# Attention and experts in one Trainium2 kernel: a quarter of the turned blocks copied on GpSimd, the first pair unturned, and a new order of the attention's instructions

## The chip, the core and the metric

The kernel runs on one core of a Trainium2 chip. The metric is the device time of one execution in microseconds, lower is better. The core's engines work through instruction streams of their own, each in order: PE (TensorE, matmuls), DVE (VectorE), ACT (ScalarE), POOL (GpSimd) and SP (SyncE), which here issues the DMA transfers. They wait for each other by semaphores.

## The reference

Attention with pooled queries (4 batches, 8 heads, 1152 keys, 576 queries after pooling pairs, head size 64), whose output is the input of a mixture of 8 experts with weights from a Sinkhorn iteration.

```python
q_pool = q.reshape(B, H, S // 2, 2, D).mean(axis=3)
scores = (1.0 / np.sqrt(D)) * np.matmul(q_pool, k.transpose(0, 1, 3, 2))
attn = np.exp(scores - np.max(scores, axis=-1, keepdims=True))
attn = attn / (np.sum(attn, axis=-1, keepdims=True) + 1e-09)
x = np.matmul(attn, v)                       # then (B * S/2, H * D) = (2304, 512)
...
P = np.exp(logits - logits.max())            # logits = x @ w_gate
for _ in range(8):                           # rows, then columns, normalized
    P /= P.sum(1, keepdims=True) + 1e-09
    P /= P.sum(0, keepdims=True) + 1e-09
    P *= N / E
for e in range(E):
    out += P[:, e:e + 1] * (np.maximum(x @ w1[e], 0.0) @ w2[e])
```

## The kernel before

The attention comes first, then the experts (`moe`, which the change leaves alone).

The attention takes two heads of a batch together, a pair; there are 16 pairs, p = 0 to 15. The 576 queries of a pair are five units: t = 0 to 3 of 128 queries for each of the two heads, and one mixed unit (t = 4) that holds the last 64 queries of both. A unit m = 5p + t goes through these steps, each a function under `unit_ops`:

- `qk` (PE, L462): scores into the PSUM tile `S`, in three parts of 384 keys; an unmixed part is six matmuls (three products of split operands, two heads). `S` has two buffers.
- `out_max` (DVE, L470): each part scaled, copied into the SBUF tile `E` and its row maximum taken; this frees `S`. `neg` (L476) takes the maximum of the three.
- `expo` (ACT, L486): the exponential in place, with row sums into `rs`.
- From here E has to be laid with keys on partitions. For most units `tr` (PE, L513, into the PSUM tile `tr`, three buffers) transposes 128x128 blocks, and `tr_out` copies them to `ET` on ACT (L523) or DVE (L525); then `av` (PE, L542) multiplies with v into the PSUM tile `av` (one buffer). The units t = 0 and 1 of the pairs 0 to 14 go another way, the turned way: `turn` (DVE, L496) transposes 32x32 blocks within each group of 32 partitions into the tile `turned`; 16 transfers `front` (SP, L554) move each of the 4x4 block quarters of 32 partitions to its place in `fronted`, four of them from a group of partitions to the same group; and `av_turned` (PE, L563) multiplies `fronted` with v, for both units in one matmul of 256 columns. Its columns are left in another order (a, t, j) in PSUM; `x_out` (ACT, L579) reads them out in the order (t, a, j), and the other two units' with a second instruction (L581). `turned` and `fronted` exist once each, so the turns of pair p + 1 need the transfers of pair p to have read, and these need `av_turned` of the pair before to be done.

Once a pair, `rec` (DVE, L588 to L591) adds 1e-9 to the nine row sums, inverts them and turns them; `spread_out` and `spread_in` carry them through DRAM to all partitions, and `x_scale` (POOL) multiplies the result. `pair_ops` loads q, k, v and splits q and k into two parts for the products (POOL additions, ACT copies).

None of this is issued in the order of the code. Each step is put into `Plan` with an engine, a cost in ns, a priority (a place in time, in units of `UNIT`), what it reads and writes, and the buffers it takes. `Plan.order` runs a list schedule over these numbers: whenever an engine is free it takes the step with the least priority value of those that are ready by its reckoning, and the engines' streams come out in that order. `STICK` favours PE steps of the same kind (`mode`) as the one before; `WAIT` is how long an engine may be held for a better step. So numbers in the table decide the streams, and on the chip each engine then follows its stream strictly.

Of the kernel before, what the change touches and what calls it, by code (L numbers as in the profile page):

```python
# [11 lines left out]
P = 128  # L12
# [151 lines left out]
class Plan:  # L164
# [9 lines left out]
    WAIT = 150  # L174
# [32 lines left out]
    def order(self):  # L207
# [31 lines left out]
        while len(out) < n:  # L239
            moved = False  # L240
            for e in engines:
# [30 lines left out]
                if e == "PE":  # L272
                    if mode and mode != o["mode"]:
                        gap = GAP_R if o["mode"] == "R" else GAP
                    mode = o["mode"]
# [35 lines left out]
TR0 = 10.0  # L311
TD = 30.0
STICK = 4.0
GAP = 145
GAP_R = 195
# [3 lines left out]
TURNED = 2  # L319

# [9 lines left out]
def attention(tc, q, k, v, w_gate, xx, ident, wg, PR, blocks, wt, dry=False, NP=NPAIRS):  # L330
# [11 lines left out]
    if not dry:  # L342
# [17 lines left out]

    def sbt(shape, dt, tag):
        return sb.tile(shape, dt, name=tag, tag=tag, bufs=caps[tag])
# [4 lines left out]
    def op(eng, cost, prio, r=(), w=(), new=(), use=(), lat=0, mode="", after=0):  # L367
        def put(fn):
            plan.op(eng, cost, prio, fn, r, w, new, use, lat, mode, after)
        return put  # L370

    def pair_ops(p):
# [6 lines left out]
        for j, (lo, hi) in enumerate(qparts):  # L379
            @op("SP", 600, T - 16 + 0.15 * j, w=[("q", p, j)], new=[] if j else [(("qr", p), "qr")], use=[("qr", p)] if j else [],  # L380
                lat=2000 + 500 * j)
# [5 lines left out]
        for j, (lo, hi) in enumerate(kparts):  # L387
            @op("SP", 600, T - 15.9 + 0.1 * j, w=[("k", p, j)], new=[] if j else [(("kr", p), "kr")],
                use=[("kr", p)] if j else [], lat=2000 + 500 * j)
# [5 lines left out]
        @op("SP", 600, T - 6, w=[("v", p)], new=[(("v", p), "vt")], lat=4000)  # L395
# [39 lines left out]
    def unit_ops(m):  # L435
# [10 lines left out]
        turns = t < TURNED and p < NP - 1  # L446
# [42 lines left out]
        if turns:  # L489
            for h in heads:  # L490
# [4 lines left out]
                def turn(h=h):  # L495
                    nc.vector.transpose(turned[:, :, :, h, t].rearrange("p b c j -> p c b j"), D["E", m][:, h].rearrange("p (c b j) -> p c b j", b=4, j=BK))  # L496
# [30 lines left out]
        new_av = t in (TURNED if p < NP - 1 else 0, QT)  # L527
        w = 64 if mixed else P
        of = t * P if not mixed else 0

        for j in range(3):
            @op("PE", 12 * (29.5 if mixed else 54.5), T + TR0 + 2.6 + 0.7 * j, mode="C",
                r=[("v", p)] + [("ET", m, g) for g in range(-(-nb // 4))],
                w=[("av", p, mixed)], new=[(("av", p, mixed), "av")] if new_av and j == 0 else [],
                use=[("v", p), ("ET", m)] + ([] if new_av and j == 0 else [("av", p, mixed)]))
            def av(j=j):
                if new_av and j == 0:
                    D["av", p, mixed] = pst([P, 512], "av")
                for c in range(3 * j, 3 * j + 3):
                    for h in range(2):  # L540
                        x = D["ET", m][:, c, 64 * h:64 * h + 64] if mixed else D["ET", m][:, h * NC + c]
                        nc.tensor.matmul(D["av", p, mixed][64 * h:64 * h + 64, of:of + w], D["v", p][:, h, c, :], x,  # L542
                                         start=(c == 0), stop=(c == NC - 1))

        if t == QT - 1 and p < NP - 1:
            @op("SP", 1, T - UNIT * (QT - 1) + 14, r=[("Y", p, i, h) for i in range(TURNED) for h in range(2)], w=[("F", p)], new=[(("F", p), "F")], use=[("T", p)])
            def room():
                pass

            for a in range(4):  # L550
                for z in range(4):
# [343 lines left out]
```

## Time and profile before

| | us |
|---|---|
| median of three runs (lowest, highest) | 1946.83 (1944.96, 1949.51) |
| the profiled execution's time | 1945.41 |
| its span, first to last instruction | 1943.5 |
| PE busy | 1910.2 (98%) |
| DVE busy | 1482.4 (76%) |
| ACT busy | 832.1 (43%) |
| POOL busy | 432.3 (22%) |

The span is what the profile's rows divide up; the time also holds what lies around it. A busy time is the union of an engine's instructions. PE's instructions overlap and their ends are modelled, so 98% says that PE nearly always had something in flight, not that it ran at its peak. The chain that ended last follows the work back from the end, at each step to what released it.

### The profile page before, as it was taken

How to read it: one execution, taken by the hardware profiler on the slowest of the kernel's cores; microseconds unless marked ns; L12 is line 12 of the kernel's file. 1: busy time of each engine (PE TensorE's matmuls, PEld its weight loads, DVE VectorE, ACT ScalarE, POOL GpSimd, SP SyncE). 2: the span in 40 equal slices, each digit the busy share in tenths (PEclk: the TensorE clock that was granted, in tenths of full speed). 3: DMA queues.
4: the chain of work that ended last, by engine and by line, in shares of the span. 5: the costliest groups of instructions: out<-in, count | busy, mean ns of one | idle time of the engine just before them, and what ended most of it. 6: DMA issues, size and time to landing. Idle time of an engine off the chain costs nothing.

```text
span 1943.5 us, 30922 instructions
## 1 busy us (share of the span) xinstructions
PE 1910.2 (98%) x11957; PEld 1681.8 (87%) x11957; DVE 1482.4 (76%) x2976; ACT 832.1 (43%) x1423; POOL 432.3 (22%) x442
## 2 busy tenths in 40 slices
PE   7999999999999999999999999999999999999999
PEld 5777777788999999999899999999989999999997
DVE  8888889878987777777867777777786777776764
ACT  5666776675433333333333333333344333333331
POOL 3222232211022212121322212121232212122210
PEclk7999999999999999999999999999999999999999
DMA  7666666522222121121312121222222121221211
GB/s 231 184 161 168 184 173 169 124 70 83 86 76 76 55 76 65 66 68 63 109 66 77 55 76 65 66 74 68 77 87 77 65 66 65 66 81 61 77 50 39
DMA packets 63221, 177.02 MB, mean 91 GB/s; under 512 B 12768, under 2 KB 22624, under 8 KB 63072
## 3 DMA queue, kind: packets, MB, share of 16 engines
q1 hardware_dynamic: 62784, 174.63, 30.3%
q8 instruction: 94, 1.54, 0.3%
q14 instruction: 55, 0.45, 0.1%
q10 hardware_dynamic: 288, 0.39, 0.1%
HBM read 134.81 MB, written 4.79 MB: 72 GB/s over the span
## 4 chain that ended last, share of the span: by engine, by line
PE 84%; DVE 8%; DMA 4%; SPq 2%; ACT 1%; issue 1%; POOL 0%; DVEq 0%; ACTq 0%
PE pso L792 39%; PE psh L754 12%; PE psh L752 12%; PE psh L753 12%; PE S L462 4%; PE av L563 3%; DVE E L470 2%; SPq L554 2%; DVE turned L496 2%; PE tr L513 2%; PE av L542 2%; DMA fronted<-turned 1%; DMA vt<-in_v_dram 1%; DVE rs L588 1%; DVE w1l L149 0%
## 5 line engine op out<-in xcount | busy, mean ns | idle before, releaser
L752 PE MATMUL psh<-xch,w1h 128*128 128x384 f32 x1344 | 451.1, 336 | 2.9 <-ACT p L767 1.5
L754 PE MATMUL psh<-xch,w1l 128*128 128x384 f32 x1344 | 449.6, 336 | 0.6 <-DVE w1l L149 0.6
L792 PE MATMUL pso<-w2h,hl 128*128 128x512 f32 x1152 | 450.1, 391 | 0.0
L792 PE MATMUL pso<-w2l,hh 128*128 128x512 f32 x1152 | 450.1, 391 | 0.0
L753 PE MATMUL psh<-xcl,w1h 128*128 128x384 f32 x1344 | 450.1, 335 | 0.0
L792 PE MATMUL pso<-w2h,hh 128*128 128x512 f32 x1152 | 448.6, 389 | 0.0
L761 ACT ACTIVATE hh<-c 128x384 fp32r<-128x384 f32 x384 | 199.8, 521 | 278.6 <-DVE c L772 277.4
L802 DVE SCALAR_TENSOR_TENSOR x<-pso,PR,x 128x512 f32<-128x512 f32 x264 | 196.9, 746 | 151.1 <-PE pso L792 150.6
L130 POOL TENSOR_TENSOR w1t<-w1s 128x256 f32<-128x256 f32 x88 | 67.0, 761 | 1031.2 <-DMA w1s<-in_moe_w_dram 836.6
L752 PEld LDWEIGHTS psh<-xch,w1h 128*128 128x128 f32 x1344 | 252.4, 188 | 9.1 <-ACT p L767 2.2
L753 PEld LDWEIGHTS psh<-xcl,w1h 128*128 128x128 f32 x1344 | 252.4, 188 | 3.5
L792 PEld LDWEIGHTS pso<-w2h,hl 128*128 128x128 f32 x1152 | 216.2, 188 | 45.1
L792 PEld LDWEIGHTS pso<-w2h,hh 128*128 128x128 f32 x1152 | 216.5, 188 | 43.1 <-ACT hh L761 0.5
L754 PEld LDWEIGHTS psh<-xch,w1l 128*128 128x128 f32 x1344 | 252.2, 188 | 1.7 <-DVE w1l L149 1.4
L792 PEld LDWEIGHTS pso<-w2l,hh 128*128 128x128 f32 x1152 | 216.3, 188 | 43.0
L470 DVE TENSOR_SCALAR_CACHE_REDUCE E<-S 128x384 f32<-128x384 f32 x432 | 219.6, 549 | 34.6 <-PE S L462 33.8
L159 ACT ACTIVATE w2h<-w2s 128x1024 fp32r<-128x1024 f32 x96 | 101.9, 1062 | 279.2 <-PE pso L792 181.3
L762 DVE SCALAR_TENSOR_TENSOR hl<-c,hh 128x384 fp32r<-128x384 f32 x384 | 211.4, 551 | 3.9 <-ACT hh L761 2.9
L486 ACT ACTIVATE E<-E,st 128x1152 f32<-128x1152 f32 x144 | 180.0, 1253 | 74.6 <-DVE st L476 70.8
L462 PE MATMUL S<-kT,qT 64*128 64x384 f32 (+1 forms) x1296 | 179.6, 372 | 22.4 <-DVE E L470 19.1
L160 DVE TENSOR_TENSOR w2l<-w2s,w2h 128x1024 fp32r<-128x1024 f32 x96 | 136.8, 1425 | 84.4 <-ACT w2h L159 84.4
L767 ACT ACTIVATE p<-psh 128x384 f32<-128x384 f32 x96 | 47.2, 491 | 331.5 <-PE psh L754 331.1
(89 smaller groups left out, 2194.6 us busy)
## 6 DMA issues: line engine op xcount, KB each, us to landing
w1s<-in_moe_w_dram SPq DMA_DIRECT2D x96, 512.0 KB
w2s<-in_moe_w_dram SPq DMA_DIRECT2D x96, 512.0 KB
fronted<-turned SPq DMA_DIRECT2D x240, 144.0 KB
qr<-in_q_dram SPq DMA_DIRECT2D x15, 640.0 KB
vt<-in_v_dram SPq DMA_DIRECT2D x16, 576.0 KB
kr<-in_k_dram SPq DMA_DIRECT2D x15, 576.0 KB
out_dram<-x SPq DMA_DIRECT2D x18, 256.0 KB
RB<-rd SPq DMA_DIRECT2D x32, 128.0 KB
```

Of the source, the lines that this page charges most:

```text
L159: self.nc.scalar.activation(out=hi, in_=self.raw2[k], func=ACTF.Copy)
L160: self.nc.vector.tensor_tensor(out=lo, in0=self.raw2[k], in1=hi.bitcast(F32), op=ALU.subtract)
L462: nc.tensor.matmul(ps[:, h, :PK], D["qT", p][rows, x, t * P:(t + 1) * P], D["kT", p][rows, y, j * PK:(j + 1) * PK], start=(i == 0), stop=( ...
L470: nc.vector.tensor_scalar(out=D["E", m][:, h, j * PK:(j + 1) * PK], in0=D["sc", m, j][:, h, :PK], scalar1=0.0625, scalar2=None, op0=ALU.mu ...
L486: nc.scalar.activation(out=x, in_=x, func=ACTF.Exp, bias=D["st", m][:, h, 3:4], accum_out=D["rs", p][:, col + h * QT:col + h * QT + 1])
L752: nc.tensor.matmul(ps, hi[:, a, c, :], blocks.xch[:, b, c, :], start=(c == 0), stop=False)
L753: nc.tensor.matmul(ps, hi[:, a, c, :], blocks.xcl[:, b, c, :], start=False, stop=False)
L754: nc.tensor.matmul(ps, lo[:, a, c, :], blocks.xch[:, b, c, :], start=False, stop=(c == 1))
L761: nc.scalar.activation(out=hh[:, fh, ts], in_=src, func=ACTF.Relu)
L762: nc.vector.scalar_tensor_tensor(out=hl[:, fh, ts], in0=src, scalar=0.0, in1=hh[:, fh, ts].bitcast(F32), op0=ALU.max, op1=ALU.subtract)
L792: nc.tensor.matmul(ps, u[:, fh, ms], w[:, fh, :], start=(n == 0), stop=(n == 11))
L802: nc.vector.scalar_tensor_tensor(out=a, in0=ps, scalar=PR[:, m, e:e + 1], in1=a, op0=ALU.mult, op1=ALU.add)
```

## The change

What it does, part by part:

- Pairs 0 and 15 go the ordinary way; only the pairs 1 to 14 have their units t = 0 and 1 turned (`spins`).
- Of the 16 quarters the four that stay on their partitions (`stay`, z = a) are copied by GpSimd; twelve transfers remain (`front`). The tiles are now `T` and `F`, taken anew for each pair from a pool with one buffer each.
- `av_turned` writes PSUM in the order (t, a, j): 256 columns in eight runs of 32. `x_out` is then one plain copy.
- 1e-9 is added by ACT (`eps`); `rec` on DVE starts with the reciprocal.
- `av` and `av_turned` are one step each for the list (three before), so nothing is put between their parts.
- The list's numbers: the loads' and transfers' costs, that a buffer read by a transfer is free only when the transfer has landed, `WAIT`, the gaps, `UNIT`, and a table `OFF` of shifts to the priorities by the step's name.

```diff
-    WAIT = 150
+    WAIT = 0
...
-                    last_use[name] = max(last_use.get(name, 0.0), end + self.FREE)
+                    last_use[name] = max(last_use.get(name, 0.0), end + self.FREE + o["lat"] * (o["eng"] == "SP"))
...
-UNIT, MIXED = 4.0, 1.8
+UNIT, MIXED = 7.6, 6.0
...
+OFF = dict(rec=20.5, q_add=-8.0, room=-38.0, qk=-2.0, stay=60.0, eps=-3.5, av_turned=43.0, expo=-12.0, spread_out=-12.0,
...
-        turned = low.tile([P, 4, NC, 2, TURNED, BK], F32, name="turned")
-        fronted = low.tile([P, 4, NC, 2, TURNED, BK], F32, name="fronted")
...
+    def done(p):
+        return [(("av", p, False), t) for t in ((0, *range(TURNED, QT)) if 0 < p < NP - 1 else range(QT))]
+
+    def lowt(tag):
+        return low.tile([P, 4, NC, 2, TURNED, BK], F32, name=tag, tag=tag, bufs=caps[tag])
...
-            plan.op(eng, cost, prio, fn, r, w, new, use, lat, mode, after)
+            plan.op(eng, cost, prio + OFF.get(fn.__name__, 0), fn, r, w, new, use, lat, mode, after)
...
-        turns = t < TURNED and p < NP - 1
+        spins = 0 < p < NP - 1
+        turns = t < TURNED and spins
...
+            if t == TURNED - 1:
+                @op("Pool", 1, T + 8, r=[("Y", p, i, h) for i in range(TURNED) for h in range(2)], w=[("G", p)], new=[(("F", p), "F")], use=[("T", p)])
+                def room():
+                    D["F", p] = lowt("F")
+
+                def runs(y, a, z):
+                    return y[BK * a:BK * a + BK, z].rearrange("p c h t j -> p (c h t j)")
+
+                for a in range(4):
+                    @op("Pool", 1300, T + 8 + a, r=[("G", p)], w=[("Z", p, a, a)], use=[("T", p), ("F", p)])
+                    def stay(a=a):
+                        nc.gpsimd.tensor_copy(runs(D["F", p], a, a), runs(D["T", p], a, a))
+
+                    for z in range(4):
+                        if z != a:
+                            @op("SP", 700, T + 8 + 0.1 * (4 * a + z), r=[("G", p)], w=[("Z", p, a, z)], use=[("T", p), ("F", p)], lat=2500)
+                            def front(a=a, z=z):
+                                nc.sync.dma_start(out=runs(D["F", p], z, a), in_=runs(D["T", p], a, z))
...
-                            nc.tensor.matmul(D["av", p, False][64 * h:64 * h + 64, :TURNED * P], D["v", p][:, h, c, :],
-                                             fronted[:, :, c, h].rearrange("p a t j -> p a (t j)"), start=(c == 0), stop=(c == NC - 1))
...
+                        nc.tensor.matmul(D["av", p, False][64 * h:64 * h + 64, :TURNED * P].rearrange("p (t a j) -> p a t j", a=4, j=BK), D["v", p][:, h, c, :],
+                                         D["F", p][:, :, c, h], start=(c == 0), stop=(c == NC - 1))
...
-                nc.scalar.activation(out=y[:, i:], in_=A[:, i:n], func=ACTF.Copy)
+                nc.scalar.activation(out=xx[:, hp, o:o + n], in_=D["av", p, mixed][:, :n], func=ACTF.Copy)
...
+            def eps():
+                y = D["rs", p][:, :2 * QT + 1]
+                nc.scalar.activation(out=y, in_=y, func=ACTF.Copy, bias=1e-9)
...
-                nc.vector.scalar_tensor_tensor(out=y, in0=y, scalar=1e-9, in1=y, op0=ALU.add, op1=ALU.max)
```

What the new numbers do to the streams shows at three places. The first is PE between two pairs, in the middle of the attention: the last unit's transposes (`tr<-ident,E`), the scores (`S<-kT,qT`), the products (`av<-ET,vt`) and the turned product (`av<-fronted` before, `av<-F` now). Before, then now:

```order
L513 MATMUL tr<-ident,E 128x128 x12
L462 MATMUL S<-kT,qT 128x384 x12
L542 MATMUL av<-ET,vt 64x128 x18
L462 MATMUL S<-kT,qT 128x384 x12
L513 MATMUL tr<-ident,E 128x128 x10
L462 MATMUL S<-kT,qT 128x384 x6
L513 MATMUL tr<-ident,E 128x128 x5
L542 MATMUL av<-ET,vt 64x128 x18
L462 MATMUL S<-kT,qT 128x384 x12
L563 MATMUL av<-fronted,vt 64x256 x18
L462 MATMUL S<-kT,qT 128x384 x12
L542 MATMUL av<-ET,vt 64x64 x18
```

```order
L542 MATMUL tr<-ident,E 128x128 x12
L470 MATMUL S<-kT,qT 128x384 x12
L542 MATMUL tr<-ident,E 128x128 x6
L571 MATMUL av<-ET,vt 64x128 x18
L581 MATMUL av<-F,vt 64x4x2x32 x18
L470 MATMUL S<-kT,qT 128x384 x12
L542 MATMUL tr<-ident,E 128x128 x9
L470 MATMUL S<-kT,qT 128x384 x12
L571 MATMUL av<-ET,vt 64x128 x18
L470 MATMUL S<-kT,qT 128x384 x12
```

The turned product now follows a product directly, the run of six scores is gone, and the fourth unit's product comes after the turned one. (A matmul of this list is one or two in the trace.)

The second place is SP in one pair of the middle: the transfers of the turned blocks, the loads of v, q and k, and the row sums' way through DRAM (`rd`, `RB`). Before, then now:

```order
L554 DMA fronted<-turned 32x1152 x3
L398 DMA vt<-in_v_dram 128x1152
L554 DMA fronted<-turned 32x1152 x13
L385 DMA qr<-in_q_dram 128x1280
L597 DMA rd<-rt 9x32 x4
L393 DMA kr<-in_k_dram 128x1152
```

```order
L525 DMA F<-T 32x1152 x12
L405 DMA vt<-in_v_dram 128x1152
L615 DMA rd<-rt 9x32 x4
L400 DMA kr<-in_k_dram 128x1152
L392 DMA qr<-in_q_dram 128x1280
```

The twelve transfers go out together and the load of v comes behind them.

The third is DVE in one pair of the middle, from the row sums to the turns (`T<-E` is the turn now). Before, then now:

```order
L588 SCALAR_TENSOR_TENSOR rs_80<-rs_80 128x9
L589 RECIPROCAL rs_80<-rs_80 128x9
L591 STREAM_TRANSPOSE rt<-rs_80 128x32
L470 TENSOR_SCALAR E,st<-S 128x384 x2
L496 STREAM_TRANSPOSE turned<-E 128x9x4x32
L470 TENSOR_SCALAR E,st<-S 128x384 x3
L496 STREAM_TRANSPOSE turned<-E 128x9x4x32
```

```order
L607 RECIPROCAL rs_81<-rs_81 128x9
L609 STREAM_TRANSPOSE rt<-rs_81 128x32
L478 TENSOR_SCALAR E,st<-S 128x384 x3
L484 TENSOR_REDUCE st<-st 128x2
L478 TENSOR_SCALAR E,st<-S 128x384
L554 COPY ET<-tr 128x512
L478 TENSOR_SCALAR E,st<-S 128x384 x4
L506 STREAM_TRANSPOSE T<-E 128x9x4x32
L484 TENSOR_REDUCE st<-st 128x2
L506 STREAM_TRANSPOSE T<-E 128x9x4x32 x3
```

Before, each turn has maxima around it; now three of the four stand in a row.

## Rows read from the trace of the kernel before

**Rows 1.** Windows by stage: busy us (instructions) of each engine, clock, DMA share, GB/s.
```profile
46.76:72.78 26.02, 24.76 (x272) 19.74 (x274) 24.37 (x71) 17.96 (x33) 7.20 (x4) 1.00 0.66 172
...
229.04:253.50 24.46, 24.46 (x272) 19.74 (x274) 21.94 (x71) 17.97 (x33) 10.21 (x6) 1.00 0.70 184
...
443.74:1943.50 1499.76, 1492.10 (x7497) 1349.69 (x7497) 1102.73 (x1836) 532.20 (x895) 307.65 (x363) 1.00 0.22 70
```

**Rows 2.** Chain that ended last, 0 to 450: start us, us, what.
```profile
63.40 2.67 DVE rs L588
...
72.78 4.04 PE av L563 x36
...
229.04 4.04 PE av L563 x36
...
253.50 4.04 PE av L563 x36
...
363.41 2.72 PE tr L63 x32
...
414.59 4.06 PE av L563 x36
```

**Rows 3.** The same chain, between the turned products of two pairs.
```profile
125.21 5.72 PE av L563 x36
...
141.87 5.26 DMA fronted<-turned
147.79 1.38 DVE turned L496
...
153.18 4.04 PE av L563 x36
```

**Rows 4.** Timeline of SP's DMA queue in that stretch.
```profile
130.98 1.80 SPq L554 DMA_DIRECT2D fronted<-turned  x3
...
133.83 8.81 SPq L554 DMA_DIRECT2D fronted<-turned  x13
```

**Rows 5.** Groups by line and form, 46.76 to 414.59: busy us, mean ns; idle before.
```profile
L433 POOL TENSOR_TENSOR kT<-kr,kT 128x1152 fp32r<-128x1152 f32 x13 | 34.9, 2688 | 20.3 <-ACT kT L428 20.3
...
L525 DVE COPY ET<-tr 128x512 f32<-128x512 f32 x44 | 30.2, 687 | 2.6 <-PE tr L513 2.5
...
L588 DVE SCALAR_TENSOR_TENSOR rs<-rs 128x9 f32<-128x9 f32 x14 | 14.7, 1053 | 0.0
...
L579 ACT ACTIVATE x<-av 128x256 f32<-128x256 f32 x14 | 5.4, 384 | 31.2 <-PE av L563 31.2
L581 ACT ACTIVATE x<-av 128x256 f32<-128x256 f32 x14 | 5.3, 379 | 0.0
```

**Rows 6.** Chain in the shortest period, 229.04 to 253.50.
```profile
233.08 1.27 PE S L462 x12
234.34 1.20 PE av L542 x36
...
238.86 0.52 PE S L462 x3
...
240.04 1.45 PE S L462 x8
241.49 1.31 PE tr L513 x12
...
244.06 2.12 PE av L542 x36
...
248.68 0.72 PE S L462 x6
```

**Rows 7.** Groups by line, 0 to 400: GpSimd's fills.
```profile
masks.py:197 POOL MEMSET ident<- 128x128 f32 x1 | 0.2, 204 | 0.3 <-POOLq L880 0.3
L356 POOL MEMSET rs<- 128x32 f32 x2 | 0.2, 124 | 0.0
```

**Rows 8.** Windows in the start, columns as in rows 1.
```profile
20.00:25.00 5.00, 3.43 (x18) 2.09 (x16) 4.72 (x12) 2.40 (x4) 3.11 (x4) 0.50 1.01 410
```

More of the change, by code (lines that the diff above doesn't have):

```diff
@@ L379, in pair_ops @@
         for j, (lo, hi) in enumerate(qparts):
[L380 to L381 removed]
+            @op("SP", 600 if first else 2600, T - 16 + 0.15 * j, w=[("q", p, j)], new=[] if j else [(("qr", p), "qr")], use=[("qr", p)] if j else [],
+                lat=2000)
             def load_q(j=j, cs=slice(lo, hi)):
@@ L525, in tr_out @@
                     nc.vector.tensor_copy(o, i)
-        new_av = t in (TURNED if p < NP - 1 else 0, QT)
+        t0 = QT if mixed else TURNED if spins else 0
+        new_av = t == t0
         w = 64 if mixed else P
         of = t * P if not mixed else 0
[L531 to L539, printed above, removed]
-                    for h in range(2):
-                        x = D["ET", m][:, c, 64 * h:64 * h + 64] if mixed else D["ET", m][:, h * NC + c]
-                        nc.tensor.matmul(D["av", p, mixed][64 * h:64 * h + 64, of:of + w], D["v", p][:, h, c, :], x,
-                                         start=(c == 0), stop=(c == NC - 1))
@@ new lines, in unit_ops, with av @@
+        A0 = ("av", p, mixed)
+        @op("PE", 36 * (29.5 if mixed else 54.5), T + TR0 + 2.6, mode="C",
+            r=[("v", p)] + [("ET", m, g) for g in range(-(-nb // 4))] + ([] if new_av else [(A0, t0)]), w=[(A0, t)],
+            new=[(A0, "av")] if new_av else [], use=[("v", p), ("ET", m)] + ([] if new_av else [A0]))
+        def av():
+            if new_av:
+                D["av", p, mixed] = pst([P, 512], "av")
+            for c in range(NC):
+                for h in range(2):
+                    x = D["ET", m][:, c, 64 * h:64 * h + 64] if mixed else D["ET", m][:, h * NC + c]
+                    nc.tensor.matmul(D["av", p, mixed][64 * h:64 * h + 64, of:of + w], D["v", p][:, h, c, :], x,
+                                     start=(c == 0), stop=(c == NC - 1))
@@ new lines, in unit_ops, with av_turned @@
+        if t == QT - 1 and spins:
+            @op("PE", 36 * 53.5 * TURNED, T - UNIT * (QT - TURNED) + TF, mode="C",
+                r=[("v", p), (A0, TURNED)] + [("Z", p, a, z) for a in range(4) for z in range(4)],
+                w=[(A0, 0)], use=[("v", p), ("F", p), A0])
+            def av_turned():
+                for c in range(NC):
+                    for h in range(2):
+                        nc.tensor.matmul(D["av", p, False][64 * h:64 * h + 64, :TURNED * P].rearrange("p (t a j) -> p a t j", a=4, j=BK), D["v", p][:, h, c, :],
+                                         D["F", p][:, :, c, h], start=(c == 0), stop=(c == NC - 1))
+                if p == NP - 2:
+                    low.release()
+                    blocks.place(tc)
@@ L649, in attention @@
         T = PAIR * NP
-        src = [("x", p) for p in range(2 * NPAIR)] + [("av", NP - 2, False)]
+        src = [("x", p) for p in range(2 * NPAIR)] + done(NP - 2)
         for n, i in enumerate((0, 1, 2, 3, 4, 6, 5)):
```

60 lines of the change are left out of this document (21 added, 39 removed).

## The prediction

> **What bounds the kernel now.** I read three views: the windows by stage, the chain that ended last, and the groups by line. The windows show that the expert stage, 443.74 to 1943.50, is PE's alone: 1492.10 of 1499.76 us busy [rows 1]. The change doesn't touch it, so all that can move lies in the 443.74 us ahead of it, the attention.
>
> There the chain shows where each turned product (`av<-fronted`) begins; there are 15, one for each of the pairs 0 to 14, and the distance from one to the next is the period of a pair: (414.59 - 72.78) / 13 = 26.29 us on the mean, and 253.50 - 229.04 = 24.46 us in the shortest [rows 2]. In that shortest one PE is busy for all of its 24.46 us, VectorE for 21.94, ScalarE for 17.97 [rows 1]. So a pair's own work on PE is 24.46 us and the other 1.8 us are waits. Two kinds stand in the chain.
>
> The first is a loop through the two buffers of the turned blocks. A turned product ends at 125.21 + 5.72 = 130.93 [rows 3]. Only then is the destination free: SP issues three transfers at 130.98, then a load of v, then thirteen from 133.83 to 142.64 [rows 4]. What waits last for them ends at 141.87 + 5.26 = 147.13; only then may VectorE overwrite the source: the next turn begins at 147.79, and the next turned product at 153.18 [rows 3]. From end to begin that is 22.25 us; with the 4.04 us of a product at full clock the loop gives 26.3 us, the mean period.
>
> The second is SCALAR_TENSOR_TENSOR on the row sums: 2.67 us on the chain at 63.40 [rows 2], 1053 ns on the mean of 14 and 14.7 us in all [rows 5], for nine columns. It sits on VectorE until ScalarE's last sum is there, with the maxima for PE's next scores queued behind it.
>
> **The sum.** It is made against the profiled execution: 1943.50 us of span, 1945.41 us of time; the median of the three runs is 1.42 us above that.
>
> *PE's own work in a pair.* The order shows the 72 paired score matmuls in six runs of 12 instead of seven runs (12, 12, 6, 12, 12, 6, 12; the run of 9 in the trace is three single-headed and six paired). Twelve take 1.27 us, six take 0.72 alone, nine take 1.45 of which three are 0.52 [rows 6]; seven runs are 5 x 1.27 + 0.72 + 0.93 = 8.0, six are 7.6. The 45 transposes and three ordinary products stay, and the turned product now follows another product. So 24.46 - 0.4 = 24.0 us.
>
> *VectorE in a pair.* It loses the SCALAR_TENSOR_TENSOR. The rest stays, so some 21.6 of 24.0 us: still less than PE. The order puts the turns together, the last three in a row: 4 x 1.38 = 5.5 us [rows 3] in which no maximum is made. Meanwhile PE has six transposes (half of twelve), a product and the turned product, 0.7 + 2.12 + 4.04 = 6.9 us [rows 2, 6], none of which needs VectorE. Margin 1.4 us. If that cover is gone, each us by which the turns are late is one of PE's.
>
> *The loop.* Twelve transfers in place of 16, with no load between them: 16 took 142.64 - 130.98 = 11.7 us, so 0.7 us each, and twelve 7.6 to 8. The loop shrinks by some 3.7 us to 18.5 + 4.04 = 22.6 us, under PE's 24.0: it no longer decides.
>
> *GpSimd's four copies.* No row shows a copy of 32 partitions on GpSimd. Below: filling 128 and 32 columns takes 204 and 124 ns [rows 7], 0.83 ns a column, so 1152 columns 1.1 us. Above: a two-input operation over 1152 columns takes 2688 ns [rows 5]. I take 1.6, nearer the fill, since one input is read and not two. GpSimd's 7.20 us in a pair [rows 1] become 11.6 to 18; either end is under 24. The copies lie beside the twelve transfers, of which the last lands about 12.5 us after the issue begins (8 and the 147.13 - 142.64 = 4.5 of the last one now); at 2.7 us each, with one addition over 640 columns that the order puts among them (1.5 at the same rate), they end at 12.3. So they cost nothing unless one takes over (24.0 - 7.2) / 4 = 4.2 us.
>
> *The ScalarE edits.* Adding 1e-9 there costs some 0.2 us, and two copies of the result (384 and 379 ns [rows 5]) become one; ScalarE has 6 us of idle in a pair. Nothing.
>
> *Waits that stay.* The new list still ties three in-order engines together. I take 0.4 us a pair (0 at best, as in the shortest pair now; 1.2 at worst, two thirds of today's 1.8). So a period of 24.4.
>
> *The start.* Up to the turned product of pair 1, at 72.78 now. VectorE is busy for nearly all of it; it loses four turns (5.5), the wait in the SCALAR_TENSOR_TENSOR (2.5), and gains copies out of PSUM: by the order six of 512 and three of 256 columns in place of five of 512, 687 ns for one of 512 [rows 5] and about 0.4 for one of 256: +1.8. Net -6.2. PE gains 36 transposes (3 x 1.31) and two products (2 x 2.12), loses a turned product (4.04), and leaves one product and six score matmuls for later: +1.4. [...] With transposes to do while VectorE works, PE stands idle less; I can't tell when the clock will rise. Bounds: 0 (it stays low as long as now, and the added work runs at half speed) to -9. I take -5.5: 67.3.
>
> *The end.* The last period now already holds work of pair 15; the new list has it behind the turned product of pair 14. By the order, 30 score matmuls (3.2), 27 transposes (2.9) and one product (2.12) move there: 8.2. Now it is 443.74 - 414.59 = 29.15 us; less some 0.5 of waits that I let go: 36.8. In turn the 13 periods lose nine transposes (1.0) and six score matmuls (0.6), and hold the gate's products, 2.72 [rows 2] and 0.3 for their transposes, once: 13 x 24.4 + 3.0 - 1.6 = 318.6.
>
> Together 67.3 + 318.6 + 36.8 = 422.7, in place of 443.74: 21.0 us less. 1945.4 - 21.0 = 1924.4, and against the median 1.4 more: **1926**, 1.1% faster.
>
> [...] The permutation that ScalarE did on its way out of PSUM is now PE's: 256 columns are accumulated in eight runs of 32 in place of one run. ScalarE's read in this pattern costs 384 ns against 379 without [rows 5], 1%; no row shows PE writing so. [...]
>
> **The rivals.**
> 1. *Slower: the scattered accumulation costs.* Turned products are 14 of 14 on PE's path, with nothing beside them. The upper price from rows: were each run of 32 charged like the smallest product here (36 of 64 columns in 1.20 us [rows 6], 33 ns), a matmul of eight runs would take 267 ns in place of 112 and the product 9.6 us: 14 x 5.6 = 78, 2004 us. It decides from 21.0 / 14 = 1.5 us more for a product of 4.04. [...] 6%.
> 2. *New waits for the old.* The margins are thin (1.4 us at the turns; scores have two buffers), and VectorE is at 90%. Then a period near 25.4 in place of 24.4: 1939. For it: only one of 13 periods is free of waits today. Against it: that one had VectorE at 21.94 of 24.46, which is as full. 15%.
> 3. *The loop is not cut:* transfers land as late as now because loads take their place on the same queues, or something else holds the buffers. Then 26.0 again: 67.3 + 13 x 26.0 + 1.1 + 36.8 = 443.2, which is today's 443.74 and the time 1946. Against it: a quarter of the bytes is gone. 4%.
> 4. *GpSimd becomes the bound,* at over 4.2 us for a copy. At 5, 27.2 us a pair: 1926 + 13 x 2.8 = 1962. The row of 2688 ns is against it. 3%.
>
> **Chances and range.** The forecast has 72%; its own range is 1918 (no waits, start at -9) to 1934 (0.8 us of waits a pair, start at -2). A measurement here tells 0.2%, 3.9 us, from no change. Faster by more: 72 + 14 from rival 2 = 86%. Within: 5% (rival 3 and the tail of 2). Slower: 9% (1 and 4). The range 1918 to 1941 leaves out rivals 1, 3 and 4, and what is faster still.
>
> **What would show it.** Right: `av<-F` begin 24.2 to 24.8 us apart and take 4.04 each; the first expert product at 420 to 426; turns that never wait for a transfer; RECIPROCAL that starts with no wait. [...]

## The result and the profile after

The changed kernel takes 1915.23 us (median of five runs, 1914.44 to 1916.61); the kernel before, beside it, 1949.51 (1944.96 to 1954.04). The ratio is 0.9827, 95% interval [0.9808, 0.9846]: 1.7% faster. The forecast was 1926 with a range of 1918 to 1941: the sign was right, and the time lies below the range; the span fell by 30.1 us (1943.5 to 1913.4) where I had worked out 21.0.

The profiled execution took 1915.23 us with a span of 1913.4 us. First the windows by stage of the kernel after (columns as in rows 1): the stretch of the thirteen periods, one period, the experts.

```profile
64.33:377.58 313.25, 313.25 (x3531) 257.88 (x3532) 278.01 (x899) 232.76 (x415) 147.88 (x102) 1.00 0.60 154
182.88:206.81 23.93, 23.93 (x274) 19.84 (x272) 21.38 (x71) 18.07 (x32) 11.62 (x8) 1.00 0.63 163
413.92:1913.40 1499.48, 1491.82 (x7497) 1349.34 (x7497) 1100.00 (x1836) 533.32 (x895) 308.19 (x363) 1.00 0.22 70
```

The experts take 1499.48 us, 0.28 less than in [rows 1]; all the rest of the difference lies ahead of them. PE is busy for all of the 313.25 us between the first and the last turned product. The timeline of the kernel after, with rows of PE, then one pair on DVE, SP and POOL:

```profile
11.48 2.29 PE L470 MATMUL S<-kT,qT 64*128 64x384 f32 x12 [0.51 <-DVE E L478]
...
17.60 0.66 PE L542 MATMUL tr<-ident,E 128*128 128x128 f32 x4
18.19 0.80 PE L470 MATMUL S<-kT,qT 64*128 64x384 f32 x6
...
21.24 1.31 PE L470 MATMUL S<-kT,qT 64*128 64x384 f32 x12
...
64.33 4.11 PE L581 MATMUL av<-F,vt 128*64 128x256 f32 x36
...
158.95 4.05 PE L581 MATMUL av<-F,vt 128*64 128x256 f32 x36
182.88 4.05 PE L581 MATMUL av<-F,vt 128*64 128x256 f32 x36
...
377.58 4.05 PE L581 MATMUL av<-F,vt 128*64 128x256 f32 x36
...
413.92 0.45 PE L772 MATMUL psh<-xch,w1l 128*128 128x384 f32 x1 [0.23 <-DVE w1l L149]
...
157.64 1.37 DVE L506 STREAM_TRANSPOSE T<-E 128x1152 f32<-128x1152 f32 x1
...
158.97 4.14 DVE L506 STREAM_TRANSPOSE T<-E 128x1152 f32<-128x1152 f32 x3
...
163.18 8.74 SPq L525 DMA_DIRECT2D F<-T  x12
...
163.23 1.14 POOL L519 COPY F<-T 32x1152 f32<-32x1152 f32 x1 [4.33 <-PE av L581]
...
165.95 3.52 POOL L519 COPY F<-T 32x1152 f32<-32x1152 f32 x3
```

Turned products stand 182.88 - 158.95 = 23.93 us apart (26.29 before on the mean, [rows 2]) and take 4.05; ten of the thirteen periods are 23.93 to 23.96, the first two 25.08 and 21.63, the one with the gate's products 27.10. The last three turns (158.97 to 163.11) run beside the product (158.95 to 163.00); twelve transfers and four copies begin as both end, and the next product comes 19.9 us later. Before, two of the four turns stood between the landing of the transfers and the product, at 147.79 [rows 3] and 150.02. Twelve scores take 2.29 us at 11.48 and 1.31 at 21.24, and six take 0.80 at 18.19: PE comes to full speed at about 17.6 us, where it was granted half from 20 to 25 us [rows 8].

Groups by form in the kernel after, 46.76 to 377.58 (columns as in rows 5); the POOL row holds all the copies:

```profile
L506 DVE STREAM_TRANSPOSE T<-E 128x1152 f32<-128x1152 f32 x53 | 70.9, 1364 | 2.0 <-ACT E L494 0.5
...
L519 POOL COPY F<-T 32x1152 f32<-32x1152 f32 x56 | 64.0, 1142 | 65.4 <-PE av L581 57.6 <-DVE st L484 5.8
...
L607 DVE RECIPROCAL rs<-rs 128x9 f32<-128x9 f32 x14 | 2.9, 209 | 0.0
```

And all that PE's matmuls waited for from 17.6 to 413.9 us (the view of the waits; us in all, times, longest):

```profile
PE av L571 <- ACT x L595: 0.7, 1, 0.7
```

### The profile page after: what moved, and what is told of

It reads as the page before. It is cut to its first block, busy times and chain, and to the rows that moved or that the text cites. A ratio compares the mean times of both kernels' runs of the same rounds, so it can differ in the third digit from the quotient of the medians.

```text
span 1913.4 us, 31073 instructions
## 1 busy us (share of the span) xinstructions
PE 1899.7 (99%) x12029; PEld 1685.5 (88%) x12029; DVE 1453.6 (76%) x2962; ACT 835.3 (44%) x1428; POOL 495.1 (26%) x498
## 4 chain that ended last, share of the span: by engine, by line
PE 75%; DVE 3%; DMA 0%; ACT 0%; issue 0%; POOL 0%; SPq 0%; ACTq 0%
PE pso L810 39%; PE psh L770 12%; PE psh L772 12%; PE psh L771 12%; DVE w1l L149 1%; DMA w2s<-in_moe_w_dram 0%; DVE xcl L100 0%; DVE x L820 0%; DVE w2l L160 0%; DVE c L790 0%; DVE hl L780 0%; ACT w2h L159 0%; DVE u L790 0%; POOL ca L754 0%; ACT hh L779 0%
## 5 line engine op out<-in xcount | busy, mean ns | idle before, releaser
L790 DVE TENSOR_TENSOR c<-psh,u 128x384 f32<-128x384 f32 x288 | 151.0, 553 | 41.2 <-PE psh L772 39.5
```

Of the source, the lines that this page charges most:

```text
L790: nc.vector.tensor_tensor(out=y, in0=ps, in1=t, op=ALU.add)
```

## The experiments

Sixteen kernels. The theories: mine (A) was that the new instructions, the twelve transfers above all, cut the loop, and that the order only keeps PE dense; the rival (B) was that the order does it. In the table "start" is where the turned product of pair 1 begins, "middle" from there to that of pair 14, "tail" from there to the first expert product (at 412.90 in after; the mark 413.92 above, like 443.74 in [rows 1], is a product of the same group 1.0 us later), all from the timeline of PE. Ratios are to the kernel before, run in the same batch; the changed kernel ran in the first batch only, so where kernels differ by 1 or 2 us I go by their traces. Before has 72.71, 341.81, 28.19.

| kernel | us | ratio [interval] | start | middle | tail |
|---|---|---|---|---|---|
| after | 1915.23 | 0.9827 [0.9808, 0.9846] | 64.33 | 313.25 | 35.32 |
| e1_sixteen | 1916.39 | 0.9835 [0.9814, 0.9857] | 65.29 | 314.39 | 35.32 |
| e2_stt | 1915.33 | 0.9829 [0.9807, 0.9851] | 65.19 | 313.22 | 35.32 |
| e3_old_parts | 1916.89 | 0.9837 [0.9815, 0.9858] | 63.44 | 314.32 | 35.31 |
| e4_new_parts | 1926.47 | 0.9889 [0.9869, 0.9909] | 70.79 | 324.80 | 27.65 |
| e5_turn_first | 1918.03 | 0.9848 [0.9824, 0.9872] | 67.34 | 313.18 | 35.31 |
| e6_copies_x4 | 1963.25 | 1.0079 [1.0058, 1.0101] | 67.82 | 355.76 | 35.32 |
| e7_runs_of_1 | 1915.88 | 0.9834 [0.9810, 0.9858] | 65.28 | 313.28 | 35.31 |
| e8_warm | 1915.30 | 0.9835 [0.9811, 0.9859] | 66.55 | 313.25 | 35.31 |
| e10_twelve | 1929.32 | 0.9915 [0.9897, 0.9932] | 70.88 | 326.80 | 28.20 |
| e11_eps | 1943.86 | 0.9980 [0.9964, 0.9995] | 69.90 | 340.38 | 27.64 |
| e12_double | 2239.15 | 1.1507 [1.1486, 1.1528] | 89.45 | 609.31 | 37.46 |
| e13_no_off | 2058.76 | 1.0579 [1.0561, 1.0598] | 66.84 | 443.22 | 44.17 |
| e14_order_alone | 1920.46 | 0.9868 [0.9852, 0.9885] | 68.11 | 314.53 | 35.32 |
| e15_unturned_old | 1942.67 | 0.9973 [0.9959, 0.9987] | 74.18 | 335.14 | 28.19 |
| e16_scratch | 1944.12 | 0.9987 [0.9977, 0.9998] | 67.59 | 339.46 | 35.32 |
| e17_old_numbers | 1930.77 | 0.9918 [0.9906, 0.9931] | 71.06 | 327.28 | 27.49 |

### Old parts in the new streams

**e1_sixteen.** In `stay` and `front` (the streams otherwise as they are):

```diff
-                        nc.gpsimd.tensor_copy(runs(D["F", p], a, a), runs(D["T", p], a, a))
+                        pass
...
-                                nc.sync.dma_start(out=runs(D["F", p], z, a), in_=runs(D["T", p], a, z))
+                                for y in (a, z) if z == (a + 1) % 4 else (z,):
+                                    nc.sync.dma_start(out=runs(D["F", p], y, a), in_=runs(D["T", p], a, y))
```

> The changed kernel with its streams as they are, but sixteen transfers again: GpSimd copies nothing, and the four quarters that stay on their partitions go by SP's queue, among the other twelve. Compared with the changed kernel (1915.23 us). Theory A (the shorter loop through the two buffers is what the change gives the middle of the attention): four more transfers at 0.7 us put some 3 us back on the loop, whose own length I put at 25.2 us, over PE's 24.08 us a pair; 13 periods by 1.1 us make it some 14 us slower, 1929, the turned products stand 25 us apart, and turns wait for a transfer. Theory B (the new order of the streams hides the loop however many transfers there are): 1915 to 1918, distance 24.1 to 24.3 us.

1916.39: B. The middle is 1.1 us longer, all of it in its first period (26.26 us in place of 25.08); most later ones are 23.92 to 23.96, as in after.

**e2_stt.** `eps` does nothing, and `rec` has its SCALAR_TENSOR_TENSOR back.

> The changed kernel with its streams as they are, but 1e-9 added by VectorE's SCALAR_TENSOR_TENSOR again, just ahead of the reciprocal and so at the new place of that step; ScalarE adds nothing. Compared with the changed kernel (1915.23 us). Theory A (the instruction itself held VectorE): 1.05 us a pair that VectorE hasn't got to spare, and PE then waits for maxima: 6 to 12 us slower over the attention, 1921 to 1927. Theory B (before, most of its duration was a wait for ScalarE's last sum, which the new place of the step doesn't have): the instruction takes 0.2 us or less, and the time stays at 1915 to 1917.

1915.33: B in the time, but the wait of before was another than B says. By the groups of e2_stt the instruction takes 166 ns, where the mean was 1053 [rows 5]:

```profile
L607 DVE SCALAR_TENSOR_TENSOR rs<-rs 128x9 f32<-128x9 f32 x13 | 2.2, 166 | 0.0
```

That mean of before is one of two kinds (least, median, greatest in the view of its line): of the 14, nine took 0.16 us and five 2.65 to 2.67. Each of the five began 0.02 to 0.04 us after one of GpSimd's additions over SBUF (L433) and ended 0.02 to 0.04 us after that addition's end, while ScalarE went on with exponentials, whose sums came at other times, the later one after the instruction's end (298.95 + 0.18 against 299.04; timeline of before):

```profile
L588 DVE SCALAR_TENSOR_TENSOR rs<-rs x16: 158/160/2669, 37.8 to 431.5; 128x9 f32<-128x9 f32 x16
...
296.34 2.66 POOL L433 TENSOR_TENSOR kT<-kr,kT 128x1152 fp32r<-128x1152 f32 x1 [1.70 <-ACT kT L428]
296.37 2.67 DVE L588 SCALAR_TENSOR_TENSOR rs<-rs 128x9 f32<-128x9 f32 x1
...
298.95 0.18 ACT L486 ACTIVATION_READ_ACCUMULATOR E<-E,st 128x1 f32 x1
```

So it was GpSimd that it waited for, not ScalarE's sum. In e14_order_alone, too, the one long one of the middle (85.20 to 87.12) ends with such an addition (at 87.10). In e2_stt GpSimd has nothing running beside twelve of the thirteen. Seven of the nine short ones of before began just as close behind the same addition, which then took 2.70 to 2.72 us in place of 2.66; why these didn't wait isn't settled.

**e3_old_parts.** Both of these, and the turned product into one run of 256 columns with the two instructions of `x_out` from before.

> The changed kernel's streams with all the old instructions in them: sixteen transfers and no copies on GpSimd, SCALAR_TENSOR_TENSOR on VectorE, PSUM written in one run of 256 columns and read out by ScalarE in two instructions with the permutation. What is left of the change is the order of the streams and the first pair unturned. Theory A: 20 to 30 us slower than the changed kernel, 1935 to 1945, so that the new order alone is worth nearly nothing against the kernel before. Theory B: 1915 to 1920, so that the order alone is nearly the whole gain. If the two parts add up, it is the sum of the two kernels beside it.

1916.89: B again. From its timeline, sixteen transfers need 11 us in place of 8.74, and the next product doesn't move for it:

```profile
159.13 4.05 PE L582 MATMUL av<-F,vt 128*64 128x256 f32 x36
...
163.44 11.00 SPq L526 DMA_DIRECT2D F<-T  x16
...
183.06 4.05 PE L582 MATMUL av<-F,vt 128*64 128x256 f32 x36
```

### New parts in the old streams

**e4_new_parts.** The kernel before, with this in `front`, and 1e-9 added by ACT behind its last sum in place of VectorE's instruction:

```diff
+                        if a == z:
+                            nc.gpsimd.tensor_copy(y, s)
+                        else:
+                            nc.sync.dma_start(out=y, in_=s)
```

> The kernel before with its streams as they are, but the new instructions in them: twelve transfers and four copies on GpSimd at the places of the four transfers, and 1e-9 added by ScalarE after its last sum. No new order, first pair turned as before, PSUM in one run. Compared with the kernel before (1949.51 us beside the changed one). Theory A: the loop falls to 22.6 us plus what the old order adds, the period from 26.3 to 24.5 to 25: 15 to 25 us faster, 1925 to 1935. Theory B: 0 to 8 us faster, since the old order puts other waits in the place of those taken away.

1926.47: now A is right. In its windows PE is busy through eight periods of 24.43 us, with no wait at all:

```profile
70.79:266.22 195.43, 195.43 (x2162) 158.29 (x2161) 174.67 (x553) 145.33 (x265) 97.56 (x66) 1.00 0.60 163
```

PE has no wait in the five periods behind these either. So the order and the instructions are substitutes: either removes the waits, and the second finds none left.

**e10_twelve** and **e11_eps.** The two edits of e4_new_parts, each alone.

> The kernel before with its streams as they are, and one thing of the change in it: twelve transfers, and four copies on GpSimd in the place of the four others. 1e-9 stays on VectorE. The two edits together took 22 us off (1926.5). Theory C (the loop through the two buffers was all that PE waited for; the time in SCALAR_TENSOR_TENSOR was waiting that came with it): 1926 to 1929, the turned products 24.4 us apart, no idle time of PE in the middle. Theory D (VectorE's wait in that instruction was a stall of its own): a half or less of the 22 us, 1935 or more.

> The kernel before with its streams as they are, and the other thing alone: 1e-9 added by ScalarE after its last sum, the SCALAR_TENSOR_TENSOR gone, sixteen transfers as before. Theory C: the loop stays at 26.3 us, 1944 to 1949, no difference to the kernel before. Theory D: 1936 to 1941.

Theory C for the most part: twelve transfers alone bring ten of the thirteen periods to 24.43 and the ratio to 0.9915; one wait of PE is left, 1.1 us in the period with the gate's products. The additions alone bring 0.2%, a small part of theory D. PE's waits in the middle (view of the waits, columns as above), in before and then in e11_eps, are nearly the same:

```profile
PE S L462 <- DVE E L470: 11.5, 12, 1.4
...
PE S L462 <- DVE E L470: 10.7, 11, 1.4
```

### The order and its numbers

**e14_order_alone.** e3_old_parts with `spins = p < NP - 1`, so that pair 0 is turned.

> The new list with every old part: sixteen transfers and no copies on GpSimd, SCALAR_TENSOR_TENSOR on VectorE, PSUM in one run with ScalarE permuting, and pair 0 turned; the list makes its streams anew for that pair. What is left of the change is the order. The same without a turned first pair took 1916.9 us, and turning the first pair again cost 2.8 us in the changed kernel. If the parts and the first pair add up: 1919 to 1921, 27 us faster than the kernel before by the order alone. If sixteen transfers need the unturned start (the loop begins a pair earlier): 1923 or more.

1920.46, as if the parts added up: the order alone, with every old instruction in it, is 1.3% faster than before.

**e17_old_numbers.** The changed code with `WAIT`, the gaps, `UNIT`, `MIXED`, `STICK`, `TR0` as before, `OFF = {}`, `TF = 26.0`.

> The changed kernel's code with the old numbers in the list (WAIT, gaps, UNIT, MIXED, STICK, TR0, no table of shifts; the turned product's priority at its old place): all the new parts, unturned pairs 0 and 15, products as one step each, in nearly the old order. The new parts alone in the old streams took 1926.5 us with a period of 24.43. If the numbers make the dense order: period 24.4, and with 3 us less at the start 1922 to 1926. If the code of the steps does (products in one piece, the list's rule that a transfer holds its buffer until it has landed): period 23.95 and 1915 to 1919.

1930.77, slower than I expected. PE has no wait in the middle, and still the period is 24.63 us by its windows:

```profile
169.62:194.25 24.63, 24.63 (x272) 19.81 (x271) 22.09 (x70) 17.92 (x33) 11.77 (x8) 1.00 0.59 161
```

So the numbers, not the code of the steps, make the 23.95: the same work in fewer runs of scores (eight a period in the trace of after, nine here). They also make most of the shorter start, 64.33 against 71.06.

**e13_no_off.** The changed kernel with `OFF = {}` and the other new numbers.

> The changed kernel with the table OFF empty: all its new instructions and rules, its pairs 0 and 15 unturned, but the list's priorities without the shifts; it makes other streams, in which VectorE's turns stand between maxima and PE's runs are split. Compared with the changed kernel (1915.23 us). If the shifts make the order that costs no wait: PE waits come back or its own work a pair grows, 1920 to 1935. If any order without the loop in it does as well: 1915 to 1918.

2058.76, far outside: 34.13 us a pair. In its timeline PE waits for maxima behind turns that stand among them, and then runs at half speed (18 scores in 3.48 us). The windows of one period show the clock at 0.85:

```profile
218.38 0.80 PE L468 MATMUL S<-kT,qT 64*128 64x384 f32 x6 [3.35 <-DVE E L476]
219.34 3.48 PE L468 MATMUL S<-kT,qT 64*128 64x384 f32 x18 [0.16 <-DVE E L476]
225.38 3.80 PE L468 MATMUL S<-kT,qT 64*128 64x384 f32 x15 [2.56 <-DVE E L476]
```

```profile
203.84:237.97 34.13, 27.91 (x273) 22.10 (x271) 24.11 (x73) 16.75 (x28) 11.64 (x8) 0.85 0.42 113
```

### The first pair

**e5_turn_first.** The changed kernel with `spins = p < NP - 1`. **e15_unturned_old.** The kernel before with `0 < p < NP - 1` in the four places that had `p < NP - 1`.

> The changed kernel with pair 0 turned again, as it was before (its units t = 0 and 1 go through the turned tiles); the list makes its streams anew with the same numbers. Compared with the changed kernel (1915.23 us), whose turned product of pair 1 begins 8.4 us earlier than before. Theory A (the start's gain is VectorE's: four turns of 1.38 us less, with PE doing transposes in their place): the four turns come back, and the full clock comes later since PE waits more: 5 to 8 us slower, 1920 to 1923. Theory B (the start's gain comes from the order, whichever way the pair goes): 0 to 2 us.

> The kernel before with pair 0 going the ordinary way, and nothing else; the list makes its streams with the old numbers. If the unturned first pair shortens the start in any order: the turned product of pair 1 begins 3 to 6 us earlier than at 72.7 and the time is 1942 to 1945. If in the old order PE then has the added transposes at half speed and VectorE's turns were not what bound the start: 0, or some us slower.

In the new order turning the first pair again costs 3.0 us of start, between the two expectations. PE is at full speed at 16.10, waits 2.77 us, and is at half again (timeline of e5_turn_first):

```profile
17.06 0.79 PE L470 MATMUL S<-kT,qT 64*128 64x384 f32 x6 [0.16 <-DVE E L478]
20.61 2.29 PE L470 MATMUL S<-kT,qT 64*128 64x384 f32 x12 [2.77 <-DVE E L478]
```

In the old order the unturned pair makes the start 1.5 us longer, not shorter: full speed comes at 15.3 us, but PE then waits for VectorE, 1.98 us up to 49.98 and 1.43 up to 52.20, and loses it: twelve scores take 2.47 us at 52.20 (timeline of PE, then windows, of e15_unturned_old):

```profile
47.00:64.00 17.00, 13.39 (x87) 10.92 (x89) 14.63 (x45) 10.71 (x20) 2.97 (x2) 0.80 0.77 181
```

Its time is still 0.3% below before, from a middle of 335.14 with 7.4 us of waits on PE; why it has fewer waits than before stays open.

### The loop in the new order

**e12_double.** Each of the twelve transfers issued twice.

> The changed kernel's streams with each of the twelve transfers issued twice (same source, same destination), 24 in all; GpSimd copies as in the changed kernel. In the changed kernel the transfers begin at the end of a turned product (163.0) and the next one begins 19.9 us later (182.9). If the loop in the new order is product, transfers, product and nothing else: 4.05 + 0.15 + 24 x 0.7 + 4.5 (the last one's way, as before) = 25.5 us against 23.95, 13 x 1.5 = 20 us slower, 1935, with PE waiting for a transfer at the turned product; the same sum gives 19.9 us with sixteen, which cost nothing. If the turns or something else stands in the loop too, more than that; if transfers queue less than their issues say, 1915.

2239.15, no test of the loop: the second transfer of a pair writes where the first does, and 21 of them take 31 us (timeline of SP's queue), with the row sums queued behind. In e16_scratch below, where they write elsewhere, 24 take 16.2 us; that the second waits for the first is my reading of these two times, no view here shows the wait itself.

```profile
201.12 31.00 SPq L526 DMA_DIRECT2D F<-T  x21
```

**e16_scratch.** The doubles into a tile of their own:

```diff
+        spare = low.tile([P, 3, NC, 2, TURNED, BK], F32, name="spare")
...
+                                nc.sync.dma_start(out=runs(spare, z, a - (a > z)), in_=runs(D["T", p], a, z))
```

> The changed kernel's streams with twelve more transfers of the same size, one behind each of the twelve, into a tile that nobody reads: 24 issues between a turned product and the next, but none that waits for another (in the kernel with each transfer done twice the second waited for the first to land, since both write the same place). If the loop in the new order is product, transfers, product: 4.05 + 0.15 + 24 x 0.7 + 4.5 = 25.5 us, 13 x 1.5 = 20 us slower than 1915, 1935, with PE waiting for a transfer at the turned product. If the queue needs longer than 0.7 us for each (24 x 147 kB in 24 us is 147 GB/s more): above 1935. If there is more slack: 1915.

1944.12. Nine of the thirteen periods are 24.8 to 25.6 us (176.47 to 201.51, say), against 25.5 by the sum; but the trace shows another loop than the sum's, so that its nearness is luck. The transfers don't begin as the product ends (180.52), they begin behind the last turn, and the first turn waits until the transfers before have landed (timelines of PE, VectorE and SP):

```profile
176.47 4.05 PE L583 MATMUL av<-F,vt 128*64 128x256 f32 x36
...
177.03 1.38 DVE L507 STREAM_TRANSPOSE T<-E 128x1152 f32<-128x1152 f32 x1 [1.80 <-DMA spare<-T]
...
178.37 4.13 DVE L507 STREAM_TRANSPOSE T<-E 128x1152 f32<-128x1152 f32 x3
...
182.58 0.54 SPq L526 DMA_DIRECT2D F<-T  x1
...
198.05 0.69 SPq L527 DMA_DIRECT2D spare<-T  x1
...
203.10 1.38 DVE L507 STREAM_TRANSPOSE T<-E 128x1152 f32<-128x1152 f32 x1 [2.83 <-issue]
```

Turns 5.5 us, transfers 16.2 (182.58 to 198.74), 4.4 to the next first turn: 26.1 from 177.03 to 203.10. So the loop that is left in the new order goes through the source of the transfers and the turns, not through the product, and PE waits for the maxima behind the turns. The first period, from 67.59 to 101.85, is 9.2 us longer than after's, which I hadn't foreseen. Groups by form, 125 to 380:

```profile
L507 DVE STREAM_TRANSPOSE T<-E 128x1152 f32<-128x1152 f32 x40 | 53.4, 1364 | 24.4 <-DMA spare<-T 11.0 <-DMA rd<-rt 7.0 <-issue 2.8
```

### The single prices

**e6_copies_x4.** `for _ in range(4):` around GpSimd's copy.

> The changed kernel with each of GpSimd's copies done four times over, same source and destination; the streams are otherwise the same. One copy took 1.14 us, four take 4.56, over the 4.2 us from which I put the bound with GpSimd. If GpSimd's work adds up (7.2 us a pair and 16 x 1.14 = 18.2, so 25.4 us, against 23.95 now): 13 x 1.5 = 19 us slower, 1934, and the turned products wait for a copy, 25.4 us apart. If the copies also hold up VectorE beside them, more: its operations of the same form last longer in the trace, and the time is above 1940. If GpSimd has more room than its busy time says: 1915.

1963.25. In the steady part the period is 26.3 us, 0.9 over the sum, and GpSimd is busy for 50.70 of 52.63 us in two of them: copies follow each other at 1.19 us, and I had left out the gaps. Other periods are longer still, the first 36.6 us, which makes the 42.5 us of the middle. VectorE waits 42.1 us for it at the turns, and PE 24.5 at the turned product. Its own instructions don't slow: turns take 1364 ns beside GpSimd's copies as after. Timeline of POOL, then the group of the turns:

```profile
163.60 4.74 POOL L520 COPY F<-T 32x1152 f32<-32x1152 f32 x4
168.31 1.56 POOL L413 TENSOR_TENSOR qr<-qr 128x640 f32<-128x640 f32 x1
169.93 14.36 POOL L520 COPY F<-T 32x1152 f32<-32x1152 f32 x12
```

```profile
L506 DVE STREAM_TRANSPOSE T<-E 128x1152 f32<-128x1152 f32 x40 | 53.5, 1364 | 43.3 <-POOL F L520 42.1
```

**e7_runs_of_1.** The turned product's output as `"p (j t a) -> p a t j"` in place of `"p (t a j) -> p a t j"`, and read out by ACT in two instructions.

> The changed kernel with the turned product written to PSUM in the order (j, t, a): neighbouring columns of a matmul lie eight elements apart, runs of 1 in place of runs of 32; ScalarE reads them out in the order wanted, in two instructions. The streams are the same. If writes out of order into PSUM cost PE nothing: a turned product stays at 4.05 us, 1915 to 1917. If scattered single elements halve the rate, a product takes 8.1 us and 14 of them 57 us: 1972. If only runs shorter than some length cost, anything between; the product's duration in the trace tells it.

1915.88; a matmul takes 379 ns (least, median, greatest in the view of the tile F), as in runs of 32:

```profile
L581 PE MATMUL av<-F,vt x288: 379/379/379, 112.0 to 283.3; 128*64 128x256 f32 x144
```

**e8_warm.** `WARM = 10`, and 3, 1 and 1 more of the same matmuls behind the first three parts of unit 0.

> The changed kernel with seven more matmuls without use on PE (128 columns, like the eight at its beginning): two more at the beginning, and three, one and one behind the first three parts of the scores of unit 0, where PE waits 1.2, 1.55 and 0.5 us for the split k and for maxima. Compared with the changed kernel, in which matmuls are at half speed from 8.8 to 17.6 us. If PE's idle time there is what keeps the clock low: full speed from about 9 to 12 us on, and as VectorE waits some 1.3 us for PE in that stretch, 1 to 1.5 us faster, 1914. If the clock doesn't follow that: 0 to 1 us slower.

1915.30: no gain. PE has hardly any idle time from 9.83 us on and is still at half speed until about 18 us (timeline of PE):

```profile
9.83 1.65 PE L363 MATMUL tr<-ident 128*128 128x128 f32 x6
...
15.36 2.29 PE L473 MATMUL S<-kT,qT 64*128 64x384 f32 x12
```

## Why the prediction was wrong

The sum was 67.3 + 318.6 + 36.8 = 422.7 us ahead of the experts. Measured: 64.3 + 313.3 + 36.3 = 413.9. That is 8.8 us; the rest of the miss of 10.8 is the 1.4 us that I added for the median and which this kernel's profiled run doesn't need, 0.3 in the experts, and rounding. Both large misses, the waits and the start, lie within the bounds that I had given them (0 and -9); it is the time that lies below the range. The range's lower end was also added up wrongly: no waits and a start at -9 give 1925.8 - 5.2 - 3.5 = 1917.1, not 1918.

**"Waits that stay: 0.4 us a pair"** is the step that failed most, 13 x 0.4 = 5.2 us. They are 0.0. I had let 0.4 of 1.8 us stay, since three in-order engines are tied together. The 1.8 wasn't all waits to begin with: PE's waits in the middle of before are 11.5 us, 0.9 a pair, and 7.2 of the 23.8 us that 13 pairs make are work that only the last two periods hold (27.51 and 28.57 us in e4_new_parts, without a wait). But the waits were the loop's, and PE had none of its own: with the loop cut, PE is busy without a gap even in the old streams (e4_new_parts). The shortest period of before, 24.46 us with no wait [rows 1], said so: a period in which the loop happened not to bind.

**"The start: -5.5"** was -8.4. Its working failed as well as its size. I took it from VectorE losing four turns. e15_unturned_old makes just that edit in the old order and the start grows by 1.5 us; e14_order_alone leaves the turns in and gains 4.6. With both it is 8.4, and the clock is likely part of how, though no run shows how much: full speed from 17.6 us on, with no idle time of PE behind it but 0.7 us near the end, where e15_unturned_old has it at 15.3 and loses it again, and e14_order_alone is granted 0.61 on the mean from 10 to 30 us. I had written that I couldn't tell when the clock, 0.50 from 20 to 25 us in before [rows 8], would rise; the bound of -9 held.

**"The loop: twelve transfers in place of 16 ... it no longer decides."** It no longer decides, but the transfers are not why. Sixteen do as well in the new order (e1_sixteen, e3_old_parts, e14_order_alone). I took what was left of the loop, 18.5 + 4.04 us, as fixed and shortened only the transfers. But it holds the stretch from the first turn behind the landing to the next transfers. Before, that runs from 147.79 to 157.25, 9.5 us, with maxima between the four turns (the last at 155.69) and the product begun behind the second. In the kernel after it runs from 157.64 to 163.18, 5.5 us, with three turns in a row and the product beside them. Timelines of VectorE and SP, before:

```profile
147.79 1.38 DVE L496 STREAM_TRANSPOSE turned<-E 128x1152 f32<-128x1152 f32 x1 [0.17 <-DMA rd<-rt]
...
155.69 1.37 DVE L496 STREAM_TRANSPOSE turned<-E 128x1152 f32<-128x1152 f32 x1
...
157.25 1.80 SPq L554 DMA_DIRECT2D fronted<-turned  x3
```

With the transfers' 8.7 us and 4.5 for the landing as before, the changed kernel's loop comes to 18.7 us; with sixteen (11.0, e3_old_parts) to 21.0; both are under 23.95, and with 24 (e16_scratch) it is 26.1 and binds. So the order takes 3.9 us off the loop, about what I had given the four transfers (3.7). That it is the place of the turns is read from these traces; no run moves the turns alone.

**"PE's own work: 24.46 to 24.0"** was right in kind and size: 23.95, by fewer runs of scores; e4_new_parts, with the old runs and no waits, has 24.43. e17_old_numbers shows that the numbers make it.

**"The end: 36.8"** was 36.3: 0.8 us of PE's waits went (1.7 before, 0.9 after) where I had let 0.5 go, and the rest is work that I had put 0.2 too high.

**"SCALAR_TENSOR_TENSOR ... sits on VectorE until ScalarE's last sum is there"** was wrong about what it waits for: the five long ones of before end with an addition of GpSimd (e2_stt). That it waits was right, and that the wait isn't its own work: 160 ns otherwise, 166 at its new place. Taking it away is worth nothing in the new order and 0.2% in the old (e11_eps). The 2.5 us that I took off the start for it can't be told from other differences: in the new order e2_stt has it back, and its start, 65.19, is that of kernels in the same streams without it (64.33 to 65.29); in the old, e11_eps without it has 69.90 and e10_twelve with it 70.88.

**GpSimd's copies** took 1.14 us, at my lower bound of 1.1, and cost nothing. **The bound with GpSimd at 4.2 us a copy** held: at 4.56 it decides, and the time is above that of before (e6_copies_x4).

Of the rivals, 1 (scattered accumulation) is refuted at both lengths of runs: a matmul of the turned product takes 379 ns at the median with runs of 32 (after) and of 1 (e7_runs_of_1), as with one run of 256 columns (before). Its 6% was my estimate; no row of before shows PE writing so. Rival 2 (new waits) didn't come: PE waits 0.7 us in all from 17.6 to 413.9. Rival 3 fell with the loop, and 4 with the copies.

What the change is worth can't be split into a sum of its parts. Alone against before: the instructions 1.1% (e4_new_parts), the order 1.3% (e14_order_alone), the unturned first pair 0.3% (e15_unturned_old), 2.7% together; all at once 1.7%. No kernel here is faster than the changed one.

## What to carry to other kernels

When a cycle through buffers sets the period, list every step on it, and what an in-order engine holds in front of each, before shortening one: here drawing the turns together beside the product did the same as a quarter fewer transfers. Waits measured while a cycle binds belong to the cycle; read what stays from a period in which it didn't bind. A sum that comes out near the measured time doesn't show its path: look in the trace at what each step waited for (e16_scratch). And look at the least and the greatest behind a mean: 1053 ns were nine times 160 and five times 2650, and what the long ones ended with was another engine than I had thought.

## What the runs showed of the hardware

- PE's full speed came between 16 and 20 us in kernels with the same streams (e3_old_parts 16.0, with a start of 63.44; e2_stt about 20, with 65.19), so differences of up to 2 us in the table's starts need not come from an edit. Idle time as in e5_turn_first (2.77 us) and e14_order_alone (2.77) was followed by half speed. Filling PE's gaps from 9.8 us on (e8_warm, full speed at about 18) didn't bring it sooner. What does isn't settled here.
- The clock's record doesn't show the beginning of every trace: in that of after it stands at 1.00 from 0 to 30 us, while twelve scores at 11.48 take 2.29 us, as at half speed.
- In the middle of before, twelve of VectorE's SCALAR_TENSOR_TENSOR with both inputs in SBUF began 0.02 to 0.04 us behind one of GpSimd's additions over SBUF. Five took 2.65 to 2.67 us and ended with it; seven took 0.16, and the addition 2.70 to 2.72 in place of 2.66. Turns beside GpSimd's copies didn't lengthen (1364 ns in after and e6_copies_x4).
- Kernels in which the loop binds vary more between runs: before 1941.7 to 1956.5 over all batches, e11_eps 1938.2 to 1948.9; after 1914.4 to 1916.6.
